# Two score products in one PSUM room, four zero fills moved to VectorE, and new instruction lists, in a gated linear attention with a maxout feed-forward block

## The chip, the cores and the metric

The kernel runs on one core of one Trainium2 chip. The core has five engines that each work through their own instructions in order: TensorE (PE in the profile, its weight loads as PEld), VectorE (DVE), ScalarE (ACT), GpSimd (POOL) and SyncE (SP, which here only issues transfers). Matrix products leave TensorE through PSUM; everything else stands in SBUF. The metric is the device time of one execution in microseconds (us), the median over runs.

## The reference

Everything is float32. Four sequences, eight heads, 768 steps, 48 channels per head; then 3072 tokens of width 384 and a hidden width of 768.

```python
mag = np.sqrt(a_re * a_re + a_im * a_im)
scale = np.minimum(mag, 0.999) / (mag + 1e-06)
a_re_n, a_im_n = (a_re * scale, a_im * scale)
...
for t in range(S):
    new_re = ar * S_re - ai * S_im
    new_im = ar * S_im + ai * S_re
    S_re, S_im = (new_re + kv, new_im)
    y[:, :, t] = np.einsum('bhd,bhde->bhe', q[:, :, t], S_re)
...
h = np.maximum(np.maximum(x @ w1, x @ w2), x @ w3)
return (h @ w_out).astype(np.float32)
```

## The kernel before

The 768 steps are cut into 12 groups of 64 (numbers 0 to 11). Each group has two tiles, x and y; a tile holds two of the four sequences with their eight heads, 128 rows of (sequence, step). Within a group the recurrence is turned into products of decayed queries and keys; between groups a state (`g`) is carried on.

The work of a group is cut into small steps, each with a short name. `SCHEDULE` is one list of 1750 such words, `name:group`, and the kernel is written out by going through it. The helper class `Bound` (line 198 is its call, so nearly every instruction of the profile has that line) ties each instruction to the one before it on its engine. So the list alone fixes the order on every engine, on the SP queue and on the POOL queue; only the waits between the engines follow from the data. Transfers are words of the list too: `Lr` and `Li` load the two parts of the gate, `Lk`, `Lq`, `Lv` keys, queries and values, `WL` the weights, `D` stores a result, and `Cd` and some others add one buffer onto another by a POOL transfer.

The words that matter below:

- `sqr`, `sqi`, `add`, `lnL`, `expe` ... `atan`, `turn`: the gate, elementwise, on ScalarE and VectorE; `af` is an absolute value.
- `sums`, `cs`, `F`: sums over steps on TensorE; `t`, `nf`, `Ek`, `Eq`, `f0` to `f3` read them out of PSUM.
- `uk`, `uq`, `tpk`, `tpq`, `Kc`, `Qc`: decayed keys and queries, their transposes on TensorE, and the copies out of PSUM.
- `A`: the scores of a tile by 32 matmuls. Head h has 80 columns, beginning at column 128 h of a PSUM room of two banks (four heads a bank).
- `g0` to `g3`: four masked copies of `A` into the tile `atm` by VectorE, one after the other.
- `B`: the scores between the halves of a chunk, by 16 matmuls with factored keys and queries (`KB`, `QB`), 128 columns; `b0`, `b1`: two ScalarE copies each from there into `atm`, behind the masked copies.
- `y`: the products of `atm` and the state with values and queries; `xx`, `xy` copy them out.
- `U`, `u`: the feed-forward products and their maximum; `S1` to `S4`, `P1` to `P7`, `r`, `o`: the output product by a Strassen scheme of seven products.
- `W..`, `T`, `M`, `J`, `O`: work at the beginning on the weights, and the output product of group 0.

PSUM is used as four rooms of two banks (a tile of 128 x 2 x 512 floats). `banks` takes the next digit of the string `SLOTS`, in list order, as the room. A room is taken over as soon as the last reader of its previous content is through. `A` takes a room for each tile and `B` takes one for both tiles of a group (in group 0 one for each tile): 258 digits.

Words in the set `OTHER` run on the engine other than the usual one: copies and absolute values on VectorE in place of ScalarE, additions on VectorE in place of a POOL transfer, loads on the POOL queue in place of SP.

Before the list begins, the kernel fills constants. In two of the `uk` tiles and both `uq` tiles the 16 columns 48 to 63 of each head's 112 are set to zero by ScalarE, as a product of a constant by 0 (line 1031); two value tiles are set to zero by VectorE.

Of the kernel before, what the change touches and what calls it, by code (L numbers as in the profile page):

```python
# [26 lines left out]
Wf6:0 nfx:0 Wb9:0 lnL:1 Enx:0 Lvy:0 csy:0 expw:1 xor:1 T2:0 relu:1 Wc9:0 We9:0 ty:0 nfy:0 mkx:0 expe:1 Wa10:0 Wf9:0
Lvx:0 Wb10:0 abs:1 Wa11:0 afx:0 sax:0 sbx:0 sumsy:0 T0:0 t0:0 mqx:0 t2:0 pw:1 Lky:1 Wb11:0 WL1:0 Lry:2 Wc10:0 half:1
Wc11:0 We10:0 ukx:0 We11:0 uqx:0 lnw:1 T1:0 Lix:2 expL:1 Wf10:0 Wa1:0 Liy:2 Wf11:0 tpqx:0 Qcx:0 mulw:1 Wb1:0 afy:0
mulai:1 tpkx:0 Wc1:0 t1:0 Fy:0 Kcx:0 kEnx:0 We1:0 WL2:0 Cdy:0 Q2x:0 Eny:0 Wf1:0 Lqx:1 lne:1 f2y:0 Q1x:0 Cdx:0 M0:0  # L30
sqi:2 Wa2:0 stt:1 Eky:0 Eqy:0 WL4:0 Wb2:0 Wa4:0 Wc2:0 Lrx:2 Wb4:0 f3y:0 We2:0 Lnop:1 f1y:0 f0y:0 say:0 Ax:0 Lqy:0
mqy:0 dkx:0 Wf2:0 g0x:0 sqr:2 sby:0 atan:1 Wg1:0 add:2 Wc4:0 lnL:2 h1x:0 QBx:0 M1:0 Lky:0 g1x:0 relu:2 turn:1 g2x:0
Wg2:0 mky:0 g3x:0 uky:0 cs:1 expe:2 WL5:0 We4:0 expw:2 M2:0 t:1 KBx:0 nfx:1 abs:2 Wa5:0 lne:2 m1:0 m0:0 uqy:0 Wb5:0
Wf4:0 Lix:3 Liy:3 Bx:0 tpqy:0 WL7:0 nfy:1 b0x:0 Wc5:0 F:1 b1x:0 sumsx:1 tpky:0 Wg4:0 xor:2 We5:0 f3:1 Qcy:0 Q1y:0 yx:0
Kcy:0 Enx:1 xx:0 Wf5:0 Q2y:0 U11x:0 Ekx:1 Eqx:1 f2:1 half:2 KBy:0 QBy:0 addw:2 Ay:0 g0y:0 Lnop:2 sumsy:1 g1y:0 f0:1
lnw:2 u11x:0 Z3:0 expL:2 f1:1 kEny:0 g2y:0 Wa7:0 af:1 Lkx:1 Wb7:0 g3y:0 Cdy:1 U01x:0 Wc7:0 mulai:2 By:0 u01x:0 b0y:0
Lqy:1 mulw:2 We7:0 Cdx:1 WL8:0 U02x:0 b1y:0 u02x:0 Wa8:0 yy:0 xy:0 sb:1 dky:0 stt:2 atan:2 h1y:0 sa:1 Wg5:0 Wf7:0
Wb8:0 U01y:0 turn:2 Wc8:0 mkx:1 U11y:0 u01y:0 u11y:0 U12y:0 Eky:1 Eny:1 mqx:1 ukx:1 U02y:0 Eqy:1 cs:2 sqi:3 uqx:1
tpqx:1 u02y:0 u12y:0 Z2:0 Lvy:1 Wg7:0 Z4:0 tpkx:1 Qcx:1 mqy:1 U21y:0 U21x:0 Lvy:2 u21y:0 We8:0 Wf8:0 Wg8:0 mky:1 Kcx:1
Q1x:1 Q2x:1 U22y:0 sumsx:2 kEnx:1 u22y:0 t:2 u21x:0 nfy:2 uqy:1 Eqx:2 Enx:2 F:2 nfx:2 Ekx:2 Ax:1 tpqy:1 f3:2 f0:2  # L40
uky:1 g0x:1 g1x:1 QBx:1 Oy:0 KBx:1 J3:0 af:2 f2:2 f1:2 Qcy:1 g2x:1 Lqx:2 mqx:2 Lvx:1 tpky:1 Q2y:1 dkx:1 QGx:1 sb:2
g3x:1 sa:2 uqx:2 Q1y:1 Lrx:3 Kcy:1 Bx:1 b1x:1 U12x:0 h0x:1 h1x:1 Lry:3 oy:0 U22x:0 b0x:1 tpqx:2 Lky:2 u12x:0 sqr:3
Qcx:2 KBy:1 Ay:1 QBy:1 u22x:0 sumsy:2 add:3 Lkx:2 g0y:1 g1y:1 g2y:1 g3y:1 Lqy:2 Eky:2 By:1 Lvx:2 yx:1 mky:2 QGy:1
kEny:1 lnL:3 xor:3 expw:3 QBx:2 xx:1 Ox:0 Eqy:2 mkx:2 Lry:4 Dy:0 expe:3 ukx:2 uky:2 b0y:1 Q1x:2 relu:3 Lrx:4 abs:3
lne:3 Lnop:3 addw:3 J1:0 Eny:2 Lqx:3 b1y:1 mqy:2 yy:1 half:3 Cdy:2 Lix:4 Cdx:2 xy:1 Liy:4 lnw:3 expL:3 J2:0 mulai:3
Lkx:3 tpky:2 kEny:2 Kcy:2 tpkx:2 Kcx:2 Lky:3 U11:1 uqy:2 u11:1 mulw:3 U01:1 tpqy:2 stt:3 atan:3 sqr:4 ox:0 h0y:1 dky:1
Q2x:2 turn:3 sqi:4 add:4 KBx:2 sumsx:3 u01:1 Qcy:2 h1y:1 cs:3 Ekx:3 h0y:2 lnL:4 Ax:2 Q2y:2 Enx:3 t:3 relu:4 kEnx:2
g0x:2 Eqx:3 Lix:5 g1x:2 nfy:3 U12:1 g2x:2 nfx:3 u12:1 g3x:2 S3:1 expw:4 U02:1 h0x:2 dky:2 af:3 F:3 expe:4 abs:4 addw:4
mqx:3 sb:3 Q1y:2 u02:1 S1:1 h1y:2 Bx:2 Lqy:3 sa:3 S2:1 Lry:5 Lvy:3 f2:3 Ay:2 b0x:2 g0y:2 P5:1 g1y:2 g2y:2 f0:3 J4:0
QBy:2 S4:1 b1x:2 P1:1 f1:3 f3:3 lnw:4 P7:1 g3y:2 QGx:2 P6:1 r1:1 sumsy:3 KBy:2 expL:4 Dx:0 r6:1 Eky:3 dkx:2 r5:1 r7:1  # L50
r57:1 Eny:3 h1x:2 By:2 yx:2 Lrx:5 xor:4 mkx:3 QGy:2 mky:3 b1y:2 ukx:3 Px:1 lne:4 Lnop:4 Eqy:3 Py:1 mqy:3 mulai:4 h0x:3
P4:1 uqy:3 uqx:3 half:4 Cdx:3 b0y:2 uky:3 P3:1 Lkx:4 Cdy:3 P2:1 xx:2 sqr:5 yy:2 xy:2 tpkx:3 Kcx:3 tpqx:3 Qcx:3 mulw:4
stt:4 U01:2 Lkx:5 Q2x:3 oy:1 Lqy:4 atan:4 Q1x:3 turn:4 ox:1 u01:2 tpky:3 QBx:3 Kcy:3 tpqy:3 F:4 Lqx:4 kEny:3 Qcy:3
QGx:3 Q1y:3 Q2y:3 sumsx:4 cs:4 f3:4 h0y:3 Liy:5 t:4 nfx:4 Ekx:4 Eqx:4 Enx:4 KBx:3 nfy:4 sqi:5 f2:4 U11:2 add:5 Ax:3
Bx:3 f0:4 Dx:1 u11:2 f1:4 lnL:5 g0x:3 mkx:4 Lvy:4 sb:4 Ay:3 mqx:4 g1x:3 af:4 g2x:3 U02:2 g0y:3 sa:4 g1y:3 g3x:3 ukx:4
relu:5 u02:2 g2y:3 Lvx:3 uqx:4 S3:2 g3y:3 KBy:3 U12:2 u12:2 b0x:3 expe:5 expw:5 kEnx:3 Lqx:6 lne:5 tpkx:4 tpqx:4 Lvx:4
dky:3 Kcx:4 S1:2 Qcx:4 dkx:3 Lky:4 sumsy:4 Eqy:4 h1y:3 S2:2 xor:5 Lry:6 Lnop:5 P1:2 Dy:1 abs:5 Eky:4 QBy:3 Lix:6 P7:2
mqy:4 P6:2 b1x:3 h1x:3 addw:5 half:5 Lrx:6 yx:3 mky:4 By:3 Eny:4 uqy:4 Cdx:4 Px:2 Py:2 lnw:5 expL:5 mulai:5 b0y:3
uky:4 Liy:6 P5:2 mulw:5 QGy:3 r1:2 xx:3 r6:2 b1y:3 S4:2 kEnx:4 P4:2 P2:2 r5:2 Cdy:4 sqr:6 sqi:6 P3:2 stt:5 atan:5
tpqy:4 Lqx:5 r7:2 r57:2 add:6 tpky:4 Qcy:4 yy:3 ox:2 dkx:4 Lix:7 Kcy:4 sumsx:5 h0x:4 turn:5 Lrx:7 Dx:2 xor:6 oy:2 xy:3  # L60
h1x:4 Q1y:4 lnL:6 Enx:5 sumsy:5 Eky:5 Ekx:5 Q1x:4 relu:6 mkx:5 cs:5 t:5 U11:3 nfx:5 expw:6 Eqx:5 Q2y:4 nfy:5 expe:6
Lky:5 mky:5 u11:3 abs:6 kEny:4 Eny:5 U01:3 af:5 Q2x:4 half:6 QGx:4 Lry:7 u01:3 Ax:4 Cdy:5 h0y:4 g0x:4 Eqy:5 g1x:4
mqx:5 dky:4 Cdx:5 F:5 g2x:4 U12:3 h1y:4 sb:5 KBx:4 QBx:4 sa:5 uqx:5 Lqy:5 U02:3 f3:5 f2:5 g3x:4 ukx:5 u12:3 uky:5
addw:6 tpqx:5 f0:5 tpky:5 u02:3 lnw:6 expL:6 f1:5 Qcx:5 Ay:4 mulai:6 Bx:4 P1:3 lne:6 Liy:7 S1:3 P5:3 mulw:6 S2:3 b1x:4
Kcy:5 g0y:4 KBy:4 b0x:4 Dy:2 sqi:7 P6:3 QBy:4 g1y:4 g2y:4 g3y:4 By:4 Lvx:5 Lky:6 mqy:5 yx:4 r1:3 S3:3 stt:6 b1y:4 P7:3
uqy:5 atan:6 tpkx:5 b0y:4 tpqy:5 QGy:4 Kcx:5 r6:3 turn:6 yy:4 Qcy:5 r5:3 r7:3 Lnop:6 sqr:7 Q1x:5 xy:4 Lkx:6 Lvy:5
h0x:5 S4:3 Q2y:5 sumsx:6 xx:4 kEnx:5 r57:3 cs:6 t:6 Ekx:6 add:7 nfy:6 Q1y:5 Py:3 nfx:6 lnL:7 P4:3 expw:7 Px:3 U01:4
QGx:5 expe:7 kEny:5 relu:7 Eqx:6 QBx:5 mqx:6 Enx:6 P2:3 af:6 Q2x:5 dkx:5 h1x:5 Liy:8 KBx:5 u01:4 sa:6 mkx:6 abs:7
sumsy:6 Eny:6 F:6 Lry:8 addw:7 oy:3 Lqy:6 U11:4 Eqy:6 P3:3 f2:6 Dy:3 f0:6 h0y:5 Eky:6 f3:6 f1:6 Bx:5 xor:7 u11:4 QBy:5
ox:3 lnw:7 sb:6 Ax:5 KBy:5 Ay:5 mqy:6 By:5 half:7 g0x:5 g1x:5 g2x:5 g3x:5 g0y:5 g1y:5 g2y:5 U02:4 Lvx:6 lne:7 b1x:5  # L70
b0x:5 yx:5 g3y:5 u02:4 expL:7 Lrx:8 mulai:7 U12:4 b1y:5 mulw:7 stt:7 Cdx:6 Lix:8 b0y:5 xx:5 atan:7 ukx:6 S3:4 P7:4
QGy:5 P1:4 tpkx:6 Kcx:6 u12:4 uqx:6 tpqx:6 Cdy:6 yy:5 mky:6 xy:5 S1:4 Qcx:6 S2:4 Dx:3 dky:5 sqi:8 r1:4 turn:7 uky:6
Q1x:6 Lnop:7 sqr:8 h1y:5 add:8 sumsx:7 kEnx:6 cs:7 t:7 P5:4 Eqx:7 P6:4 Px:4 S4:4 Py:4 P4:4 P2:4 Lvx:7 xor:8 Ekx:7
Lkx:7 P3:4 lnL:8 r6:4 uqy:6 nfy:7 r5:4 r7:4 r57:4 nfx:7 expe:8 Enx:7 tpqy:6 tpky:6 h0x:6 Lqx:7 F:7 expw:8 relu:8 mqx:7
af:7 Lvy:6 Lky:8 ox:4 Qcy:6 QBx:6 dkx:6 oy:4 Dy:4 mkx:7 Lix:9 Q2y:6 U11:5 abs:8 Dx:4 QGx:6 half:8 f0:7 Q1y:6 h1x:6
KBx:6 Kcy:6 sb:7 sa:7 f2:7 U01:5 ukx:7 U12:5 Q2x:6 kEny:6 uqx:7 f3:7 addw:8 h0y:6 u01:5 Lrx:9 u11:5 f1:7 u12:5 dky:6
# [988 lines left out]
```

## Time and profile before

| | |
|---|---|
| median of 3 timed runs | 553.96 us (553.03 to 554.14) |
| the profiled execution's own time | 549.62 us |
| its span, which the profile divides | 547.9 us |
| mean granted TensorE clock in it | 0.983 |
| transfers in it | 47.93 MB, mean 87 GB/s |

The profile page gives, for one execution, the busy time of each engine, the span in 40 slices (each digit the busy tenths of a slice), the chain of work that ended last, and groups of instructions of one kind with their count, their summed time and the mean of one. Other views of the trace give the busy time in chosen stretches, the instructions in order of time, and who waited for whom. Times count from the beginning of the span. The 1.72 us between the span and the execution's own time belong to neither engine. The rows themselves stand where the prediction uses them.

### The profile page before, as it was taken

What the parts mean: (1) busy time and instruction counts of PE and PEld (TensorE: products, weight loads), DVE (VectorE), ACT (ScalarE), POOL (GpSimd) and SP (SyncE); (2) the same over time, 40 slices, a digit from 0 to 9 for tenths busy, and PEclk for the clock granted to TensorE, in tenths of its full rate; (3) what the DMA queues carried; (4) which work ended last, traced back from release to release, by engine and by line L of the source; (5) the groups of instructions that cost most, each with busy time, mean ns of one, the idle gap of its engine ahead of it and who ended that gap; (6) DMA issues with size and microseconds to landing.
All of it is one profiled execution on the core that took longest, in us unless ns stands there. A gap on an engine that the chain in (4) does not pass through costs nothing.

```text
span 547.9 us, 22377 instructions
## 1 busy us (share of the span) xinstructions
PE 512.3 (94%) x9998; PEld 439.4 (80%) x9998; DVE 484.2 (88%) x730; ACT 367.4 (67%) x575; POOL 119.9 (22%) x173
## 2 busy tenths in 40 slices
PE   2469889999999999999999999999999999999997
...
DVE  6999989999999999999999969998999996977234
ACT  7999988779858878689585558756567578211100
...
GB/s 240 270 203 197 183 155 57 90 91 130 45 76 75 106 81 53 159 63 61 91 21 186 32 17 102 90 67 74 97 68 25 75 105 1 4 44 4 2 0 58
DMA packets 113983, 47.93 MB, mean 87 GB/s; under 512 B 100832, under 2 KB 106400, under 8 KB 113888
## 3 DMA queue, kind: packets, MB, share of 16 engines
...
q14 instruction: 17, 0.14, 0.1%
...
## 4 chain that ended last, share of the span: by engine, by line
PE 72%; DVE 12%; ACT 6%; DMA 4%; issue 3%; SPq 2%; POOL 0%; DVEq 0%; ACTq 0%
PE up L198 28%; PE op L198 22%; PE y L198 6%; PE A L198 4%; PE dk L198 3%; PE tp L198 3%; SPq L198 2%; PE sums L198 2%; DVE xhx L198 2%; ACT L198 2%; PE F L198 1%; PE cs L198 1%; PE B L198 1%; DMA q<-in_q_dram 1%; DVE uk L198 1%
## 5 line engine op out<-in xcount | busy, mean ns | idle before, releaser
L198 PE MATMUL up<-xhx,w 128*128 128x256 f32 x792 | 177.7, 382 | 0.0
L198 PEld LDWEIGHTS up<-xhx,w 128*128 128x128 f32 x792 | 148.4, 190 | 23.4 <-issue 1.2
L198 ACT ACT_TABLE_LOAD x53 | 68.0, 1283 | 4.5 <-issue 3.6
L198 POOL DMA_DIRECT2D ar<-nf x44 | 41.9, 1382 | 85.8 <-DVE ar L198 82.7
L198 PE MATMUL op<-wo,xhx 128*128 128x192 f32 (+1 forms) x220 | 49.2, 362 | 0.0
L198 DVE TENSOR_TENSOR Q<-Q,f 112x1024 f32<-112x1024 f32 (+1 forms) x48 | 44.9, 949 | 0.1
L198 ACT COPY atm<-B 32x128 f32<-32x128 f32 x96 | 24.6, 256 | 29.9 <-DVE atm L198 22.8
L198 PE MATMUL y<-atm,vb 128*32 128x64 f32 x1152 | 39.0, 221 | 0.8 <-issue 0.8
L198 PEld LDWEIGHTS op<-wo,xhx 128*128 128x128 f32 x220 | 36.7, 190 | 3.4 <-ACT xhx L198 0.6
L198 DVE TENSOR_TENSOR xhx<-xhx,up 128x768 f32<-128x768 f32 x22 | 20.9, 950 | 19.7 <-PE up L198 19.6
L198 PEld LDWEIGHTS y<-atm,vb 128*32 128x32 f32 x1152 | 32.9, 109 | 5.0 <-issue 3.1
L198 PE MATMUL y<-QG,g 112*32 112x64 f32 x1408 | 36.7, 218 | 0.0
L198 DVE TENSOR_TENSOR ot<-ot,op 128x192 f32<-128x192 f32 (+1 forms) x66 | 27.1, 416 | 9.7 <-PE op L198 7.0
L198 PEld LDWEIGHTS y<-QG,g 112*32 112x32 f32 x1408 | 34.3, 109 | 0.0
L198 PE MATMUL op<-wo,strassen 128*128 128x192 f32 x176 | 32.9, 330 | 0.0
L198 PE MATMUL op<-w,strassen 128*128 128x192 f32 x176 | 32.5, 329 | 0.3 <-issue 0.3
L198 PE MATMUL A<-Q,K 112*32 112x80 f32 x1536 | 30.8, 234 | 1.4 <-issue 1.3
L198 DVE COPY_PREDICATED atm<-masko,A 128x256 f32<-128x256 uint8 x72 | 30.2, 432 | 1.3
L198 PEld LDWEIGHTS A<-Q,K 112*32 112x32 f32 x1536 | 27.3, 110 | 4.8 <-issue 3.1
L198 ACT ACTIVATE xhx<-up 128x768 f32<-128x768 f32 x16 | 13.0, 811 | 27.0 <-PE up L198 27.0
L198 PEld LDWEIGHTS op<-w,strassen 128*128 128x128 f32 x176 | 29.0, 190 | 2.0 <-issue 1.0
L198 PEld LDWEIGHTS op<-wo,strassen 128*128 128x128 f32 x176 | 28.9, 190 | 1.7 <-ACT e L198 0.6
...
## 6 DMA issues: line engine op xcount, KB each, us to landing
...
```

The lines of the kernel that those rows point to most:

```text
L198: ins = f(*a, **kw)
```

## The change

Four edits, made together:

1. `B` no longer has a room. `A` and `B` of a tile share one, taken by whichever of the two comes first in the list. `B` writes the 32 columns behind the 80 of `A`, for the four heads of the first bank, and `b0`, `b1` read them there.
2. The four zero fills are VectorE memsets.
3. `SCHEDULE` is another list of the same 1750 words, and `SLOTS` another string, of 245 digits.
4. `OTHER` is another set.

```diff
@@ scores
         if name == "A":
-            ps = T["A", x] = banks("A")
+            ps = once(("A", x), lambda: banks("A"))
...
         elif name == "B":
-            g, c_ = divmod(x, C)
-            ps = T["B", x] = once(("Bp", g if g > 0 else -x), lambda: banks("B"))[:, c_:c_ + 1]
+            ps = once(("A", x), lambda: banks("A"))
...
-                        mm(out=ps[o:o + 32, 0, i * 32:i * 32 + 32], lhsT=T["KB", x][0:DD, 2 * h + j],
+                        mm(out=ps[o:o + 32, 0, i * P + 80:i * P + 112], lhsT=T["KB", x][0:DD, 2 * h + j],
...
-            src = T["B", x][:, 0, 0:4 * 32].rearrange("p (h t) -> p h t", h=4)
+            src = T["A", x][:, 0].rearrange("p (h t) -> p h t", h=4)[:, :, 80:112]
@@ before the list
     for t in us["k"][:2] + us["q"]:
-        act.mul(t[:, :, D:L64], biases[:, 0:1].to_broadcast([P, H * (L64 - D)]).rearrange("p (h d) -> p h d", h=H), 0.0)
+        dve.memset(t[:, :, D:L64], 0.0)
@@ SCHEDULE, its first words
-Lrx:0 sqr0:0 Lix:0 Zf:0 CL:0 sqi0:0 add0:0 Liy:0 sqi1:0 Zg:0 lnL0:0 Lry:0 WL0:0 sqr1:0 add1:0 expe0:0 expw0:0 lne0:0
+Zf:0 Lix:0 sqi0:0 Lrx:0 Lry:0 sqr0:0 sqr1:0 add0:0 lnL0:0 Liy:0 sqi1:0 Zg:0 xor0:0 WL0:0 xor1:0 WL3:0 expe0:0 expw0:0
...
@@ OTHER
-abs0:0 Lkx:0 Lqy:1 Lqx:1 Wg4:0 Wg8:0 Lkx:2 Lqx:3 Lvy:1 abs:3 addw:3 Lkx:3 Lky:3 Lvy:3 u11:2 addw:5 Lvy:4 Lvx:5 Lqx:5
-u01:3 abs:6 Lvy:5 Lkx:6 u11:4 Lvx:6 Lvy:6 addw:7 Qcx:6 Lky:6 Lkx:7 u11:5 af:7 u01:5 Lky:7 xx:6 Kcx:7 af:8 Lqx:8 Kcy:7
-Lqx:9 xx:7 xy:7 u01:7 af:9 abs:10 Lvx:8 Lqx:10 Lvx:9 af:10 Lqx:11 Qcy:9 Lvx:10 abs:11 Kcx:10 Lqy:10 xx:9 Lkx:11 Lvy:10
-xx:10 xy:10 Qcy:11 Kcx:11 Lvy:11 Kcy:11
+abs0:0 Lkx:0 Lqx:0 afx:0 Lvx:0 Wg4:0 Lqy:1 u01x:0 Lvy:1 Wg8:0 Lqx:2 Lvx:2 Lqy:2 addw:3 af:3 Lqy:3 Lkx:3 Lqx:4 af:4
+Lvy:3 Lqx:6 Lvx:3 Lqx:5 Lkx:5 abs:6 addw:6 af:5 Lqy:5 Kcx:5 Lkx:6 af:6 addw:7 Lky:6 Qcy:6 af:7 addw:8 u11:5 xx:6 Lvy:8
+af:8 Lky:8 Lvx:8 xx:7 Qcy:8 u11:7 Lkx:9 af:9 Lvy:9 Lqy:10 Lvx:9 abs:11 xx:9 addw:11 Lky:11 Lky:10 af:11 xx:10 Kcy:11
+Lvx:11
```

Of the new lists the change says that they were made for several draws of the times at which transfers land. Old and new differ nearly everywhere in the order of single words; the products that TensorE computes are the same. Where `B` stands among the masked copies, in list order:

| tile | before | after |
|---|---|---|
| x of group 0 | A g0 g1 g2 g3 B | A g0 g1 g2 B g3 |
| y of group 4 | A g0 g1 g2 g3 B | A g0 g1 g2 B g3 |
| y of group 6 | A g0 g1 g2 g3 B | A g0 g1 B g2 g3 |
| y of group 10 | A g0 g1 g2 g3 B | A g0 B g1 g2 g3 |
| x of group 4 | A g0 g1 g2 g3 B | B A g0 g1 g2 g3 |
| x of group 8 | A g0 g1 B g2 g3 | B A g0 g1 g2 g3 |

Over all 24 tiles of the changed list, `B` stands behind at least one masked copy of its own tile in 12, and ahead of all of them in the other 12.

More of the change, by code (lines that the diff above doesn't have):

```diff
@@ L27 @@
[L27 to L76, printed above, removed]
@@ new lines @@
+Ax:1 g0x:1 g1x:1 g2x:1 g3x:1 uky:1 mqx:2 tpqy:1 Ekx:2 Qcy:1 Oy:0 sqi:3 Lrx:3 Q1y:1 QBx:1 Lry:3 Q2y:1 af:2 tpky:1 sb:2
+QGx:1 dkx:1 Lky:2 KBx:1 oy:0 Bx:1 kEny:1 h0x:1 Kcy:1 U12x:0 b1x:1 KBy:1 U22x:0 h1x:1 QBy:1 b0x:1 Lqy:2 mkx:2 sa:2
+u12x:0 sqr:3 Ay:1 uqx:2 By:1 add:3 ukx:2 u22x:0 g0y:1 g1y:1 xor:3 lnL:3 relu:3 expw:3 yx:1 sumsy:2 Eqy:2 Eky:2 Eny:2
+expe:3 g2y:1 mky:2 g3y:1 lne:3 abs:3 Ox:0 Lky:3 b1y:1 QGy:1 mqy:2 tpqx:2 uqy:2 Lnop:3 half:3 uky:2 Lrx:4 b0y:1 yy:1
+Qcx:2 tpky:2 tpqy:2 ox:0 J3:0 xy:1 tpkx:2 addw:3 Cdy:2 Q1x:2 Cdx:2 xx:1 J1:0 lnw:3 expL:3 Q2x:2 kEny:2 mulw:3 Kcx:2
@@ new lines @@
+xor:4 Lvx:3 mulai:4 By:2 Eky:3 half:4 mulw:4 yx:2 stt:4 Eqy:3 sa:3 sb:3 xx:2 Px:1 P3:1 Cdy:3 b0y:2 QGy:2 Cdx:3 Py:1
+b1y:2 P2:1 atan:4 mky:3 sqi:5 Eny:3 P4:1 ukx:3 uqx:3 mqy:3 yy:2 xy:2 tpkx:3 Kcx:3 tpqx:3 uqy:3 U01:2 Qcx:3 oy:1 u01:2
+uky:3 QGx:3 turn:4 ox:1 Q1x:3 tpqy:3 Qcy:3 tpky:3 Kcy:3 kEnx:3 QBx:3 h0y:3 F:4 f3:4 sumsx:4 Q2y:3 cs:4 f2:4 Lrx:5
+Lkx:5 f1:4 h0x:3 sqr:5 Ekx:4 Q2x:3 t:4 f0:4 nfy:4 KBx:3 Lkx:4 nfx:4 Enx:4 Eqx:4 Q1y:3 sb:4 af:4 kEny:3 Dy:1 sa:4 Lvy:4
+U11:2 Lqx:4 mqx:4 Bx:3 add:5 Ax:3 lnL:5 Ay:3 g0x:3 mkx:4 u11:2 U02:2 g0y:3 g1x:3 expw:5 expe:5 g1y:3 relu:5 ukx:4
@@ new lines @@
+u02:2 g2x:3 g2y:3 lne:5 U12:2 g3x:3 S3:2 b0x:3 abs:5 Lry:6 uqx:4 Lky:4 b1x:3 tpkx:4 Kcx:4 addw:5 u12:2 Lix:6 xor:5
+tpqx:4 Qcx:4 dky:3 g3y:3 sumsy:4 Eky:4 Lvx:4 dkx:3 h1y:3 P7:2 Eny:4 S1:2 mky:4 KBy:3 S2:2 P5:2 P6:2 half:5 P1:2 Lqy:4
+QBy:3 h1x:3 kEnx:4 lnw:5 expL:5 S4:2 r1:2 By:3 Dx:1 b1y:3 Lrx:6 yx:3 b0y:3 Lnop:5 Px:2 P2:2 Py:2 mulw:5 mulai:5 Eqy:4
+uky:4 P4:2 r6:2 r5:2 QBx:4 r7:2 QGy:3 stt:5 P3:2 Lqy:5 tpky:4 Cdy:4 atan:5 Cdx:4 mqy:4 r57:2 sqr:6 uqy:4 Lqx:5 oy:2
+tpqy:4 Qcy:4 yy:3 Lky:5 KBx:4 Kcy:4 dkx:4 turn:5 xx:3 ox:2 xy:3 sumsy:5 Liy:6 h0x:4 kEny:4 sumsx:5 h1x:4 Eny:5 Enx:5
```

123 lines of the change are left out of this document (79 added, 44 removed).

## The prediction

> **What bounds the kernel now.** First the page: its totals and its slices.
>
> ```profile
> span 547.9 us, 22377 instructions
> PE 512.3 (94%) x9998; PEld 439.4 (80%) x9998; DVE 484.2 (88%) x730; ACT 367.4 (67%) x575; POOL 119.9 (22%) x173
> ...
> PE   2469889999999999999999999999999999999997
> DVE  6999989999999999999999969998999996977234
> ACT  7999988779858878689585558756567578211100
> ```
>
> TensorE is full from the seventh slice on. Ahead of that VectorE and ScalarE are full and TensorE is not. VectorE stays at nine tenths to the middle. The view of stretches, cut at two places that I explain next, gives the idle time:
>
> ```profile
> 0.00:14.00 14.00, 3.09 (x36) 2.15 (x37) 9.75 (x27) 9.90 (x21) 11.20 (x41) 1.00 0.90 241
> 14.00:84.80 70.80, 52.65 (x824) 36.40 (x823) 68.47 (x105) 67.78 (x110) 25.90 (x30) 0.88 0.93 199
> 84.80:237.70 152.90, 151.00 (x3372) 129.63 (x3376) 148.61 (x218) 120.72 (x184) 36.79 (x46) 1.00 0.45 87
> 237.70:540.00 302.30, 301.73 (x5750) 267.69 (x5751) 254.24 (x378) 169.01 (x263) 46.04 (x57) 1.00 0.28 56
> 540.00:547.90 7.90, 3.86 (x24) 3.56 (x22) 3.09 (x7) 0.00 (x0) 0.00 (x0) 0.92 0.19 51
> ```
>
> The columns are the length, then the busy time of PE, PEld, DVE, ACT and POOL. From 84.8 to 540 us TensorE is idle for 2.5 us in all. Nothing but later or earlier readiness of its inputs can move the end, and what is lost ahead of 84.8 us is lost for good. VectorE's idle time is 4.25 us in the first 14, 2.33 in the next 70.8, 4.29 to 237.7: 10.9 together, so up to there it is almost a second bound. Behind 237.7 it idles 48 us.
>
> The two cuts are checkpoints. In both lists the same TensorE words stand ahead of `tpqx:1` (transposes of tile x, group 1) and again ahead of `sumsx:6`, in other orders. As the products are the same, the time at which these two begin says how the kernels stand.
>
> **The change part by part.**
>
> *The zero fills.* In order of time, with the piece of the chain of waits that leads in:
>
> ```profile
> 1.58 3.84 DMA ai<-in_a_im_dram
> ...
> 4.92 0.51 ACT L198 ACTIVATE uk<-biases 128x128 f32<-128x128 f32 x2
> 5.33 0.49 ACT L198 ACTIVATE uq<-biases 128x128 f32<-128x128 f32 x2
> 5.73 0.51 ACT L198 ACTIVATE e<-ar 128x384 f32<-128x384 f32 x1
> 6.68 0.66 DVE L198 CUSTOM_DVE_ANT_0 L<-L,e 128x384 f32<-128x384 f32 x1 [2.62 <-ACT L L198]
> 7.08 0.52 ACT L198 ACTIVATE L<-ai 128x384 f32<-128x384 f32 x1 [0.43 <-DMA ai<-in_a_im_dram]
> 7.51 0.51 ACT L198 ACTIVATE L<-L 128x384 f32<-128x384 f32 x1
> ```
>
> The four products take ScalarE 0.81 us (4.92 to 5.73). But the first square of the new list needs `ai`, which lands at 1.58 + 3.84 = 5.42; the third needs SP's third load, for which ScalarE waited until 7.08; the logarithm behind it starts at 7.5 as before. So removing them gains nothing, and ScalarE's idle start grows by 0.81. On VectorE the four memsets, 0.17 each by a memset of the same size (row below), lie in the 2.62 us ahead of 6.68. Without that cover they would cost 0.66. The first addition comes some 0.3 earlier (5.42 + 2 x 0.46 for two squares = 6.3).
>
> *ScalarE to the first checkpoint.*
>
> ```profile
> 81.53 0.65 ACT L198 ACTIVATE hT<-up 128x256 f32<-128x256 f32 x2
> 84.25 0.50 ACT L198 ACTIVATE E<-sums 128x384 f32<-128x384 f32 x1
> ...
> 83.40 0.94 DVE L198 TENSOR_TENSOR uq<-CS,q 128x768 f32<-128x768 f32 x1
> 84.80 0.66 PE L198 MATMUL tp<-ident,uq 64*112 64x64 f32 x16 [0.20 <-ACT E L198]
> ```
>
> The transposes start at 84.80, when `Eqy:1` on ScalarE frees their room (ends 84.75); `uqx:1` on VectorE ended at 84.34. In the old order 133 ScalarE instructions stand ahead of this point, in the new one 125. Gone are the four fills (covered, nothing), `afx:0` (0.51 by the square of that size) and `u01x:0` (0.33, half of the first row), both now VectorE's; and `Eky:1` and `Eqy:1`, two exponentials that now stand behind the checkpoint (0.4 each, as they follow one another). Sum 0.51 + 0.33 + 0.8 = 1.6 us sooner.
>
> *VectorE to both checkpoints.* Its rows:
>
> ```profile
> L198 DVE COPY_PREDICATED atm<-masko,A 128x256 f32<-128x256 uint8 x72 | 30.2, 432 | 1.3
> L198 DVE COPY_PREDICATED atm<-maskd,A 128x512 f32<-128x512 uint8 x24 | 17.4, 728 | 2.1 <-PE A L198 2.1
> L198 DVE TENSOR_TENSOR w<-w,L 128x768 f32<-128x768 f32 x13 | 12.4, 950 | 0.7 <-ACT L L198 0.7
> L198 DVE CUSTOM_DVE_ANT_0 L<-L,e 128x768 f32<-128x768 f32 (+1 forms) x13 | 11.7, 899 | 3.0 <-ACT L L198 2.6 <-issue 0.4
> L198 DVE SCALAR_TENSOR_TENSOR w<-w,ar 128x768 f32<-128x768 f32 (+1 forms) x13 | 11.6, 890 | 1.3 <-DMA ar<-nf 1.3
> L198 DVE TENSOR_TENSOR strassen<-xhx,strassen 128x512 f32<-128x512 f32 x11 | 7.5, 683 | 7.5 <-PE op L198 7.5
> L198 DVE COPY K<-tp 112x1024 f32<-112x1024 f32 x5 | 6.1, 1216 | 0.3 <-PE tp L198 0.3
> L198 DVE TENSOR_SCALAR xhx<-up 128x768 f32<-128x768 f32 x6 | 5.6, 946 | 0.0
> L198 DVE TENSOR_TENSOR hT<-hT,up 128x256 f32<-128x256 f32 x6 | 2.4, 409 | 0.0
> L198 DVE TENSOR_SCALAR af<-nf 128x768 int32<-128x768 int32 x4 | 2.2, 552 | 0.0
> L198 DVE TENSOR_SCALAR L<-ar 128x768 int32<-128x768 int32 x4 | 2.2, 550 | 0.0
> L198 DVE MEMSET upto<- 128x128 f32 x1 | 0.2, 165 | 0.0
> ```
>
> To `tpqx:1` VectorE gets `afx:0` (0.28, half of an `af`), `u01x:0` and `u12y:0` (0.41 each) and loses one weight step (about 0.55): +0.55, less 0.3 for the earlier start. If none of its later waits shrank it would be ready at 84.34 + 0.3, and the gain would be 0.2 us; if they do, ScalarE's 1.6 is the limit. Range 0.2 to 1.6.
>
> To `sumsx:6` the new order has these ahead that the old one has not: four memsets (0.66, in idle time), `afx:0` 0.28, `u01x:0` 0.41, `af:3 af:4 af:5` 1.66, `addw:6` 0.95, `S4:3` 0.68, `turn:6` 0.89, `add:7` 0.90, `Kcx:5` 1.22: 7.7. Not ahead any more: `abs:3` 0.55, `u11:2` 0.95, `addw:5` 0.95, `u01:3` 0.95: 3.4. Net 4.3, and I take 4.0 since each starts a little before the one ahead of it ends. How near was VectorE?
>
> ```profile
> 234.45 1.22 DVE L198 TENSOR_TENSOR QG<-Q,f 112x1024 f32<-112x1024 f32 x1
> ...
> 235.94 1.72 PE y L198 x112
> 237.66 0.81 PE sums L198 x16
> ```
>
> The last that counted was `QGy:4`, ending at 235.67, with `yy:4` (1.72) still between it and the sums. In the new order it is `Kcx:5`, directly ahead of the sums. So they gain 237.6 - 235.67 = 1.9 of room. Start: 235.7 + 4.0 = 239.7, less the covered memsets and the earlier start (0.66 + 0.3): 238.7, which is 1.1 later than before. Against that stand waits of VectorE up to here:
>
> ```profile
> DVE atm L198 <- PE A L198: 1.5, 1, 1.5
> DVE nf L198 <- ACT t L198: 1.2, 2, 1.0
> ```
>
> Both are for engines that were late because ScalarE was. With ScalarE 1.6 sooner I take 2.3 of these 2.7 us as gone: 238.7 - 2.3 = 236.4, 1.2 us sooner than 237.6. Bounds: 1.1 later with none gone; ScalarE's 1.6 sooner.
>
> *Behind it.* TensorE is idle 0.6 us in the next 302, so the difference stays. VectorE has 48 idle us there, and the new `OTHER` takes work off it (relu by `xhx<-up` six to two, `K` copies five to two). At the end both lists finish with the last product, one addition and a store:
>
> ```profile
> 543.89 0.56 DVE L198 TENSOR_TENSOR ot<-ot,op 128x384 f32<-128x384 f32 x1 [0.56 <-PE op L198]
> ```
>
> Nothing changes there. The leftover `kEny:11` stood behind that addition, beside the store; its successor `kEnx:11` stands ahead of it, in idle time.
>
> *The shared room.* Thirteen fewer rooms are taken. But the built order of the changed kernel has waits that the old one lacks: where `B` stands behind a masked copy, its first matmul waits for that copy, and the next copy waits for `B`, although the columns are different. In-order TensorE then holds all products behind `B`. The copies of a tile take 0.73 + 3 x 0.43 = 2.02 us; `B` stands behind at least one of them in 12 tiles. I take 0: in six of the 12, eleven or more words of the list lie between the copy and `B`, and in the other six one to five; only those six are near. Bounds: 0, and one copy in each, 12 x 0.43 = 5.2.
>
> [...]
>
> **The sum.** 547.9 - 1.2 = 546.7 for the span, 549.62 - 1.2 = 548.4 for that execution. The median of the runs shown is 4.3 us above the profiled one; I carry the difference over: 553.96 - 1.2 = 552.8.
>
> **The rivals.**
>
> *VectorE takes ScalarE's place* and none of its waits shrink: +1.1, 555.1. For it: 68.47 of 70.80 and 148.61 of 152.90 us busy, and +4.0 of work moved forward. Against: its waits for the scores and for `t` are ScalarE's lateness.
>
> *Slower: `B` locked to the masked copies.* In 12 tiles TensorE stops for one copy: 5.2 - 1.2 = +4.0, 558.0. It decides from six such tiles on (6 x 0.43 = 2.6 eats the gain and the margin). For it: a VectorE with under 3% idle time reaches its copies late. Against: the distance in the list, which leaves just six near cases.
>
> *Landing times.* The timed runs take 4.3 us more than the profiled one, and transfers are 0.90 and 0.93 busy in the first two stretches. If that excess is waiting for transfers, and the new list is proof against it: 549.6. For it: the chain passes a landing of over five us in the second stretch.
>
> ```profile
> 38.97 5.53 DMA ar<-in_a_re_dram
> ```
>
> Against: ScalarE and VectorE were busy for all but 3.0 and 2.3 of the 70.8 us there, so the landing cost them little.
>
> *The change doesn't do what it says:* the freed rooms and the new order only move the waits about, 553.96.
>
> **How the numbers follow.** Forecast 0.36 (its own range 551.8 to 553.6), VectorE 0.26, locked `B` 0.16, landing times 0.14, nothing 0.08. Within 0.2% (1.1 us), what a measurement here can't tell from no change, lie a quarter of the forecast, a third of the VectorE case and the last: 0.09 + 0.09 + 0.08 = 0.26. Faster: 0.27 + 0.14 = 0.41. Slower: 0.17 + 0.16 = 0.33. The range goes from just under the landing case to just under the locked one, 549.2 to 557.8.
>
> **What would show it.** Right: `tpqx:1` begins at 83.2 to 84.6 and `sumsx:6` near 236.4, VectorE's idle time up to there falls from 10.9 us, and the first addition on VectorE stands at about 6.4 with the memsets ahead of it. Wrong: `sumsx:6` at 238.7 or later with VectorE idle as before; or waits of `A<-QB,KB` for `atm` on VectorE in a dozen tiles; or a gain that arises behind 237.7 us, where I see none.

## The result, and the profile after

| | before | after |
|---|---|---|
| median of 20 timed runs each | 552.32 us (550.71 to 554.46) | 556.02 us (551.49 to 559.24) |
| the profiled execution's own time, and its span | 549.62, 547.9 | 552.38, 550.5 |

The ratio is 1.0062, with a 95% interval of 1.0042 to 1.0082: slower, by 3.7 us between the medians, where the forecast was 1.2 us faster. The spread has changed too: these 20 runs of the kernel before lie within 4 us, those of the changed one cover 8.

The stretches of the changed kernel, cut where the prediction cut them (the columns are again the length, then the busy time of PE, PEld, DVE, ACT and POOL):

```profile
0.00:14.00 14.00, 3.11 (x36) 2.18 (x37) 10.17 (x31) 9.34 (x17) 11.20 (x41) 1.00 0.89 236
14.00:84.80 70.80, 53.66 (x827) 37.26 (x828) 68.52 (x107) 67.12 (x107) 27.57 (x33) 0.86 0.93 201
84.80:237.70 152.90, 149.62 (x3304) 128.57 (x3306) 149.00 (x217) 118.52 (x183) 38.38 (x48) 1.00 0.43 84
237.70:540.00 302.30, 300.75 (x5818) 266.18 (x5807) 247.66 (x371) 175.31 (x271) 41.51 (x49) 1.00 0.28 54
540.00:550.50 10.50, 6.13 (x36) 5.56 (x34) 4.09 (x8) 0.00 (x0) 0.00 (x0) 0.99 0.14 38
```

TensorE's idle time in the third stretch is 3.28 us (1.90 before), in the fourth 1.55 (0.57 before). VectorE's up to 237.7 is 3.83 + 2.28 + 3.90 = 10.0 us (10.9 before). What ended TensorE's idle time behind 84.8 us, by the view of waits (us in total, how often, the longest):

```profile
PE y L198 <- issue: 2.4, 2, 1.5
PE A L198 <- issue: 0.6, 1, 0.6
PE tp L198 <- PE y L198: 0.5, 1, 0.5
PE A L198 <- DVE KB L198: 0.4, 1, 0.4
PE up L198 <- issue: 0.3, 1, 0.3
```

The large ones are not for another engine. "issue" is time in which the engine waited for nothing that the profile shows. In the timeline such a stop can lie inside a word, between two products of the same kind, where the trace shows no wait for an input:

```profile
67.97 0.73 PE L198 MATMUL F<-cuts,Ln 64*48 64x29 f32 x46
73.56 0.60 PE L198 MATMUL F<-cuts,Ln 64*48 64x29 f32 x18 [4.85 <-issue]
```

These are two rows of `F:1` from a second profiled execution of the changed kernel (first experiment below). In the first execution the same word breaks after the same 46 products, and `yx:1` breaks at 106.8:

```profile
68.20 0.73 PE L198 MATMUL F<-cuts,Ln 64*48 64x29 f32 x46
70.49 0.41 PE L198 MATMUL F<-cuts,Ln 64*48 64x29 f32 x18 [1.56 <-issue]
...
106.78 0.22 PE L198 MATMUL y<-QG,g 112*32 112x64 f32 x1
108.47 0.24 PE L198 MATMUL y<-QG,g 112*32 112x64 f32 x1 [1.47 <-issue]
```

What sits at these places? The page's part on DMA queues has a row that the prediction passed over:

```profile
q8 instruction: 78, 1.28, 0.9%
```

78 packets, 1.28 MB: 16384 bytes each in the trace. TensorE's stream in the trace (products, weight loads and the sequencer's own rows, in order of time) has 20126 instructions, 258 for each packet. Numbering the stream shows that behind 84.8 us every one of these stops stands at an instruction whose number is 193 plus a multiple of 256. I call these places boundaries. One stretch between two of them:

```profile
218.30:231.50 13.20, 12.62 (x255) 11.02 (x255) 12.86 (x20) 11.16 (x18) 1.55 (x2) 1.00 0.44 85
```

255 products and 255 weight loads; with two rows of the sequencer they are 512, two blocks of 256. Five of the stops and the packets on that queue, worked out from the first profile (times in us):

```
instruction   last start   next start   packet before it: begins, takes   next start behind its end
  1217          68.73        70.49        68.09   0.88                       1.52
  2753         106.78       108.47       106.24   0.99                       1.24
  7617         217.63       218.34       216.00   0.93                       1.41
  8129         230.77       231.57       229.30   0.92                       1.35
 16321         430.45       431.63       429.15   0.99                       1.49
```

These numbers fit instructions of TensorE that come in blocks of 256, each by one packet (0.88 to 1.51 us in this profile, 0.96 in the median). That of a block begins only around the time at which TensorE passes the boundary before it: in these five rows 0.9 to 3.2 us behind it, elsewhere in this profile up to 4.0 ahead. In the five rows TensorE went on 1.24 to 1.52 us after the packet had ended. The blocks that end at these five stops hold dense words (in this profile 112 products of `y` start within 1.7 us, 64 of `A` in 1.1) and lasted 2.5 to 4.1 us: they were used up before the next one was there. I call these stops fetch stops, and count one where at a boundary the gap between two starts is over 0.25 us and over the usual spacing of such products, and the packet ended 1.1 to 2 us before.

In this profile 7 of 78 boundaries stop TensorE. They cost it 6.95 us, and the experiments show lists in which such stops cost far more (up to 30.3 us, with 128 instructions ahead).

### The profile page after: what moved, and what is told of

Same layout as the page of the kernel before. It is cut to its first block, busy times and chain, and to the rows that moved or that the text cites. A ratio compares the mean times of both kernels' runs of the same rounds, so it can differ in the third digit from the quotient of the medians.

```text
span 550.5 us, 22367 instructions
## 1 busy us (share of the span) xinstructions
PE 513.3 (93%) x9998; PEld 439.8 (80%) x9998; DVE 479.4 (87%) x730; ACT 370.3 (67%) x575; POOL 118.7 (22%) x169
## 3 DMA queue, kind: packets, MB, share of 16 engines
q8 instruction: 78, 1.28, 0.9%
## 4 chain that ended last, share of the span: by engine, by line
PE 80%; DVE 8%; ACT 4%; issue 3%; DMA 2%; SPq 2%; ACTq 0%; DVEq 0%
PE up L198 32%; PE op L198 22%; PE y L198 7%; PE A L198 6%; PE tp L198 4%; PE dk L198 4%; SPq L198 2%; PE sums L198 2%; PE F L198 1%; DVE xhx L198 1%; DVE Q L198 1%; DVE w L198 1%; PE cs L198 1%; DMA xhx<-in_moe_w_out_dram 1%; DVE atm L198 1%
## 5 line engine op out<-in xcount | busy, mean ns | idle before, releaser
L198 PE MATMUL up<-xhx,w 128*128 128x256 f32 x792 | 177.4, 382 | 0.4 <-issue 0.3
L198 PEld LDWEIGHTS up<-xhx,w 128*128 128x128 f32 x792 | 148.6, 190 | 23.4 <-DVE g L198 1.3
L198 POOL DMA_DIRECT2D ar<-nf x44 | 44.3, 1471 | 58.0 <-DVE ar L198 56.1
L198 DVE TENSOR_TENSOR Q<-Q,f 112x512 f32<-112x512 f32 (+1 forms) x48 | 44.8, 953 | 4.4 <-ACT Q L198 4.4
L198 PE MATMUL op<-wo,xhx 128*128 128x192 f32 (+1 forms) x220 | 48.7, 363 | 0.0
L198 ACT COPY atm<-A 32x128 f32<-32x128 f32 x96 | 24.5, 256 | 34.3 <-DVE atm L198 29.9
L198 PEld LDWEIGHTS op<-wo,xhx 128*128 128x128 f32 x220 | 36.8, 190 | 5.7 <-ACT xhx L198 0.9
L198 PE MATMUL y<-atm,vb 128*32 128x64 f32 x1152 | 39.5, 221 | 1.0 <-issue 1.0
L198 DVE TENSOR_TENSOR xhx<-xhx,up 128x768 f32<-128x768 f32 x22 | 20.9, 950 | 20.6 <-ACT xhx L198 11.1
L198 PE MATMUL y<-QG,g 112*32 112x64 f32 x1408 | 37.1, 218 | 1.5 <-issue 1.5
L198 PEld LDWEIGHTS y<-atm,vb 128*32 128x32 f32 x1152 | 33.1, 109 | 4.8 <-issue 4.0
L198 PEld LDWEIGHTS y<-QG,g 112*32 112x32 f32 x1408 | 34.4, 109 | 1.6 <-issue 1.6
L198 DVE TENSOR_TENSOR ot<-ot,op 128x192 f32<-128x192 f32 (+1 forms) x66 | 27.1, 418 | 8.8 <-PE op L198 6.3
L198 POOL DMA_DIRECT2D Ln<-e x11 | 14.2, 1294 | 94.9 <-ACT e L198 88.4
L198 ACT ACTIVATE xhx<-up 128x768 f32<-128x768 f32 x20 | 16.1, 807 | 27.0 <-PE up L198 26.9
L198 DVE COPY_PREDICATED atm<-masko,A 128x256 f32<-128x256 uint8 x72 | 30.8, 435 | 2.4 <-PE A L198 1.3
L198 PE MATMUL op<-wo,strassen 128*128 128x192 f32 x176 | 32.7, 328 | 0.0
L198 PE MATMUL op<-w,strassen 128*128 128x192 f32 x176 | 32.5, 329 | 0.0
L198 ACT ACTIVATE E<-sums 128x384 f32<-128x384 f32 x48 | 22.6, 491 | 13.8 <-PE sums L198 9.9
L198 PE MATMUL A<-Q,K 112*32 112x80 f32 x1536 | 30.3, 234 | 1.7 <-ACT K L198 1.5
L198 PEld LDWEIGHTS op<-wo,strassen 128*128 128x128 f32 x176 | 29.1, 190 | 1.5 <-issue 0.8
```

The costliest lines, as they stand in the source:

```text
L198: ins = f(*a, **kw)
```

## The experiments

Theory F in what follows: the loss is made of fetch stops. Its rivals change from run to run and are named in the expectations. "Small products" are matmuls of 3 x 3 elements on a constant, which put four instructions each into TensorE's stream: with 32 of them the page counts 10062 products and 10062 weight loads, 64 more of each. The edit for 32:

```diff
+    pad = psum.tile([P, 2, 512], FP, tag="ps3", name="pad")
+    for _ in range(32):
+        mm(out=pad[0:3, 0, 0:3], lhsT=biases[:, 0:3], rhs=biases[:, 0:3], start=True, stop=True)
     program(SCHEDULE, 0)
```

**The changed kernel again** (no edit).

> The changed kernel once more, for a second profiled execution and its spread beside the others. Theory F (instruction fetch): in the first profile TensorE stopped 6.7 us in all (before: 2.6) at instructions 193 + 256 j of its stream, in the middle of words, where a transfer of 16 KB on the instruction queue had ended only 1.2 to 1.5 us earlier. Then the same boundaries (tiles F near 70.5, yx:1 near 108, U02:3 near 218, By:4 near 231, yx:9 near 431, tpqx:11 near 485) stop again, by amounts that differ by tenths, 6 to 10 us in all, and the ratio is 1.004 to 1.008. Theory W (late inputs): the stops are waits for VectorE or ScalarE that the profile failed to name; then they come and go with those engines and are not bound to the instruction's number.

Measured: 1.0043 (1.0013 to 1.0073), 550.8 to 558.9 us. This profile fell on a long execution: 558.89 us, span 557.1. It stops at six boundaries, 11.75 us in all, against 6.95 at seven in the first. Five of the six expected places stop again (not the one near 485, which stands in `tpkx:11` and not in `tpqx:11`), and there is a new stop of 1.7 us at 280. The stop in `F:1` is 5.06 us instead of 1.76. The two executions differ by 6.6 us in span, and 4.8 of it are fetch stops.

**128 instructions ahead of either list** (the edit above, on the changed kernel and on the one before).

> The changed kernel with 32 products of 3 x 3 elements ahead of everything on TensorE, at a time when it idles: they cost nothing by themselves, and move the boundaries of the 256-instruction blocks by 128 instructions. Theory F: no stop where the stops were (108, 218, 231, 431); new ones in the middle of words near 105.5, 139, 148, 171, 199.5, 212, 224, 233 and some ten later places, since 23 blocks instead of 12 now last less than 3.3 us; the time is 3 to 9 us longer than the changed kernel's, 1.011 to 1.022 of the kernel before. Theory W: the stops stay in their words, and the time is the changed kernel's within 0.3%.

> The kernel before with the same 32 products ahead. Theory F: 25 blocks instead of 11 last less than 3.3 us, so 3 to 9 us longer, 1.006 to 1.016. Theory W: 1.000 within 0.002.

Measured: 1.0443 (1.0402 to 1.0485) and 1.0483 (1.0454 to 1.0512), some 20 and 26 us more than the same lists without the small products. The sign and most of the places are Theory F's, the size is more than twice what it expected at most. The waits of the padded new list:

```profile
PE A L198 <- issue: 8.3, 8, 1.4
PE y L198 <- issue: 4.4, 4, 1.9
PE dk L198 <- issue: 3.4, 3, 1.3
PE F L198 <- issue: 2.3, 2, 1.2
PE tp L198 <- issue: 1.8, 1, 1.8
```

They have moved to other words. `F:1`, which broke after 46 products, is whole, and a later word, `By:0`, breaks instead:

```profile
68.53 0.92 PE L198 MATMUL F<-cuts,Ln 64*48 64x29 f32 x64
...
72.38 0.34 PE L198 MATMUL A<-QB,KB 112*32 112x32 f32 x17 [0.58 <-DVE atm L198]
74.48 0.33 PE L198 MATMUL A<-QB,KB 112*32 112x32 f32 x15 [1.76 <-issue]
```

There are 24 fetch stops, 30.3 us, in the padded new list, and 18 stops, 25.6 us, in the padded old one.

**256 instructions ahead** (64 small products on the changed kernel). If the small products themselves cost, this costs more than 32 of them; if the boundaries do, they are back in place.

> The changed kernel with 64 of the small products ahead: 256 instructions, one whole block, so that the boundaries fall where the changed kernel has them, one block later in number. Theory F: the stops are back at yx:1, By:4, the words of 270 to 280 us, yx:9, four to seven in all, 5 to 12 us; 1.004 to 1.009 of the kernel before, though twice as many products stand ahead as in the run with 32 (1.044). Rival C (the small products themselves, or the time TensorE starts, are what costs): more than with 32, 1.04 to 1.09.

Measured: 1.0127 (1.0087 to 1.0167), against 1.0443 with half as many. Nine stops, 8.2 us in the profiled execution (555.65 us), and `F:1` breaks again after 46 products:

```profile
70.56 0.73 PE L198 MATMUL F<-cuts,Ln 64*48 64x29 f32 x46
72.08 0.45 PE L198 MATMUL F<-cuts,Ln 64*48 64x29 f32 x18 [0.79 <-issue]
```

The ratio is above Theory F's 1.009 and far below the rival's 1.04. With this it is shown that the places of the boundaries set the loss: half a block ahead costs one and the same list some 20 us, a whole one 4. What the 4 are made of is open.

**12 instructions ahead** (3 small products, on the changed kernel and on the one before).

> The changed kernel with 3 of the small products ahead instead of 32: the boundaries move by 12 instructions. From the durations of the blocks alone the stops would be about a tenth less than the changed kernel's (sum of shortfalls below 3.9 us per block 18.1 instead of 20.0). Theory F: same places as the changed kernel, or one word earlier, 0.5 to 2 us less, 1.000 to 1.007. If 12 instructions already cost as much per instruction as 128 did: 1.008 or more, which would mean that the small products themselves cost and not the boundaries.

> The kernel before with 3 of the small products ahead, 12 instructions. By the durations of its blocks this is near its best place (sum of shortfalls below 3.9 us 11.7 instead of 16.1). Theory F: the stop near 70 us (1.5 to 2.8) goes or shrinks, and nothing over 1 us comes in its place: 0.995 to 1.000. Rival C: 1.001 to 1.005.

Measured: 1.0029 (1.0009 to 1.0048) for the changed kernel, 549.95 to 554.89 us, and 1.0060 (1.0039 to 1.0081) for the one before. In the first `F:1` is whole and there is no fetch stop ahead of 84.8 us; 7.7 us remain behind:

```profile
68.43 0.92 PE L198 MATMUL F<-cuts,Ln 64*48 64x29 f32 x64
```

The times no longer reach to 559. So the stop in `F:1`, 1.0 to 5.1 us in six profiles of lists that have it there, probably makes much of the changed kernel's spread. The second was a miss: the early stop stayed at 1.5, and two of 1.3 and 0.9 came at 146 and 278. The durations of blocks alone, from which I had expected a gain, foretell the sign of the large step of 128 but not single stops.

**Words moved** (four places in the list of the changed kernel).

```diff
-dky:4 U02:3
+U02:3 dky:4
-By:4 uqy:5 xx:4 atan:6 g3y:4 b1y:4 Lvx:5 sqr:7 P6:3
+P6:3 By:4 uqy:5 xx:4 atan:6 g3y:4 b1y:4 Lvx:5 sqr:7
-yx:9 S1:8 S2:8 f0:10 xx:9 P6:8
+S1:8 S2:8 f0:10 P6:8 yx:9 xx:9
-U12x:0 b1x:1 KBy:1 U22x:0 h1x:1 QBy:1 b0x:1 Lqy:2 mkx:2 sa:2 u12x:0 sqr:3 Ay:1 uqx:2 By:1
+b1x:1 KBy:1 h1x:1 QBy:1 b0x:1 Lqy:2 mkx:2 sa:2 sqr:3 Ay:1 uqx:2 By:1 U12x:0 U22x:0 u12x:0
```

> The changed kernel with seven words of its list moved by a few places, so that a word with long products stands inside the block of 256 instructions that ends in a stop: U12x:0 and U22x:0 (with u12x:0) from ahead of Ay:1 to behind By:1 (stop of 1.7 us near 108), U02:3 ahead of dky:4 (0.7 near 218), P6:3 ahead of By:4 (0.8 near 231), P6:8 ahead of yx:9 and xx:9 (1.2 to 1.7 near 431). Work and engines are the same. Theory F: these four stops, 4.4 to 5.0 us, shrink to under 1.5 in all, and the time falls by 2 to 5 us, to 0.995 to 1.001 of the kernel before. Rival S (the new order itself is the loss: late VectorE, held rooms): the stops change their place but the time stays at 1.003 to 1.008.

Measured: 1.0098 (1.0061 to 1.0135). All four stops are gone: behind 84.8 us 0.9 us of stops remain, of 5.2 and 6.7 in the two profiles without the moves. But the time did not fall. Waits for other engines stand in their place:

```profile
PE A L196 <- ACT atm L196: 1.2, 1, 1.2
...
PE up L196 <- DVE g L196: 1.1, 1, 1.1
...
PE op L196 <- DVE strassen L196: 1.2, 1, 1.2
```

(The first rows of the view of waits for 84.8 to 130, 215 to 232 and 425 to 445 us; L196 is the line L198 of the other kernels.) The span less its fetch stops is 550.8 us, over 5 more than without the moves. This run can't tell the theories apart: a word moved by a few places meets inputs that aren't there yet. A smaller move, one word, on top of the 3 small products:

```diff
-P7:4 u12:4 h0y:5 tpqx:6 tpkx:6 Lix:9 Kcx:6 yy:5
+u12:4 h0y:5 tpqx:6 tpkx:6 Lix:9 Kcx:6 yy:5 P7:4
```

> The changed kernel with 3 of the small products ahead (1.0029 by itself, with stops of 1.8 and 1.6 us near 274 and 278) and one word, P7:4, moved from ahead of tpqx:6 to behind yy:5, so that eight long products stand between the short ones there. Theory F: these two stops shrink to under 0.5 each, if the transposes that now come 1.4 us earlier don't wait for VectorE: 0.997 to 1.000 of the kernel before. If they do wait, the time is as without the move, 1.001 to 1.005.

Measured: 1.0049 (1.0028 to 1.0069). One of the two stops is gone (278), the other (1.7 at 274) is not, and the time is no better. No version made here beats the kernel before.

**Small products at the end** (320 of them behind the last word; a single execution).

> The changed kernel with 320 of the small products behind its last word, when no load is under way: 1280 instructions, five blocks, on a TensorE that has nothing else. Theory F: they don't run at their own rate (256 of them in under 2 us) but at the rate of the fetches, one stop per block, 3.5 to 4.5 us for each, 15 to 22 us in all. Theory W: no stop among them, 7 to 10 us in all.

Measured: no stop among them. The 1280 instructions take 16.1 us, 3.2 us a block, and that is their own rate: the products start 50 ns apart, at a granted clock of 0.65 in the first half of that stretch and 0.50 in the second. So the time lies in Theory F's range without the stops that were to make it, and above Theory W's. The run was meant to be dense and wasn't; it tells only that in this stretch, at 3.2 us a block and with no load under way, the transfers kept up. The queue has 83 packets, five more than without the five blocks, so it is TensorE's.

**The first two edits by themselves.** The fills alone, in the kernel before:

> The kernel before with the zero fills alone, by VectorE. The prediction's cost of this edit: 0, hidden in VectorE's 2.62 us of idle time and ScalarE's wait for its input: 0.999 to 1.001. The other end of its bounds: 0.66 us later, 1.001. TensorE's instructions are the same, so Theory F has its stops where the kernel before has them.

Measured: 0.9998 (0.9980 to 1.0016). The shared room and the fills, in the old lists:

```diff
+            if g in (3, 4, 9):
+                ps, w, o_ = once(("Bp", g), lambda: banks("B"))[:, c_], 32, 0
+            else:
+                ps, w, o_ = once(("A", x), lambda: banks("A"))[:, 0], P, 80
```

`SLOTS` keeps 226 of its digits; the rest had to change because rooms are now held at other times.

> The old lists, unchanged, with the first two edits alone: the zeroes by VectorE, and the second score product in the free columns of the first one's room, in nine of the twelve groups (in groups 3, 4 and 9 the old order leaves no room free, so they keep the room of their own). Instructions on TensorE stay the same in number and order. Theory F, and the prediction's cost of 0 for both edits: 0.999 to 1.002. The rival that the second score product is locked to the masked copies: 9 tiles' worth of 0.43 us, 1.003 to 1.008, with waits of TensorE for atm.

Measured: 1.0363 (1.0342 to 1.0384), 20 us more. Its fetch stops are 5.7 us, so most of the loss has another source. TensorE's waits behind 84 us:

```profile
PE A L196 <- DVE atm L196: 6.1, 3, 3.1
PE tp L196 <- DVE ot L196: 2.1, 2, 1.9
PE y L196 <- ACT Q L196: 1.6, 1, 1.6
...
PE tp L196 <- ACT atm L196: 1.2, 1, 1.2
PE tp L196 <- ACT K L196: 1.1, 1, 1.1
```

The first fits TensorE at a room that the masked copies still read; rows of `tp` waiting for what others write fit rooms that come free late. How much is the shared room and how much the changed digits was not separated.

**A weight load issued later** (the word `WL5` from ahead of `g0x:0` to behind `F:1`, with its steps and those of `WL8` behind it), to find out why the packet ahead of `F:1`'s break is so late.

> The changed kernel with one weight load of 768 KB, WL5, issued some 6 us later in the list (behind F:1 instead of ahead of g0x:0, 64.8 us in the first profile), and the steps that use it and the load WL8 behind it moved back with it. TensorE's list is untouched, so the boundaries stay in their words. Theory L (the fetch of the block that ends in F:1 is late because loads fill the transfer engines, share 1.00 to 1.03 behind the boundary near 64): the share there falls, the fetch begins under 2 us behind the boundary instead of 3.2 and 6.8 us, and the stop in F:1, 1.8 and 5.1 us in two profiles, is under 0.8. Rival: the fetch is late for another reason, then the stop in F:1 stays between 1.5 and 5 us. In both, later weights can cost some us near 100 us, where U12x:0 and U22x:0 need them, so the whole time tells little: 0.998 to 1.012.

Measured: 1.0372 (1.0350 to 1.0395); the load was issued at 82.9 us, 18 later than in the changed kernel and not 6, and the late weights cost 11.9 and 6.8 us at two products, as the expectation had feared but not sized. For the question itself: the stop in `F:1` is still 1.65 us, a miss for Theory L. The stretches behind the boundary at 63.6 (the last two columns are the transfer engines' share and GB/s):

```profile
64.50:65.00 0.50, 0.50 (x7) 0.50 (x7) 0.50 (x1) 0.50 (x2) 0.00 (x0) 1.00 1.24 240
65.00:65.50 0.50, 0.48 (x5) 0.29 (x3) 0.50 (x2) 0.50 (x1) 0.00 (x0) 1.00 1.05 203
65.50:66.00 0.50, 0.29 (x16) 0.29 (x20) 0.50 (x2) 0.50 (x3) 0.00 (x0) 1.00 0.73 135
66.00:66.50 0.50, 0.50 (x41) 0.50 (x34) 0.50 (x2) 0.50 (x3) 0.00 (x0) 1.00 0.02 0
```

Even without `WL5` the transfer engines are full to 65.9, and the packet begins at 66.5. In the 557.1 us execution they are full past 70.6, and it begins at 70.68. That fits a packet that waits behind loads, as does the delay of packets behind their boundary: up to 7.4 us between 53 and 75 us, 0.8 in the median behind 90 us. Against it, in the run with one word moved and 3 small products the packet began only 0.5 us behind the boundary at 63.8, though the transfer engines were full (1.09 and 1.44 in the half microseconds on either side). So why the packets are late is open; no run here had that stretch free of loads.

**The profiles of the two lists together** (those with words moved, rooms changed or products at the end left out). The span less the fetch stops:

| profile | span | fetch stops to 84.8, behind | the rest |
|---|---|---|---|
| old list | 547.9 | 1.5, 0.6 | 545.7 |
| old list, fills by VectorE | 551.4 | 2.8, 0.5 | 548.1 |
| old list, 3 small products | 551.8 | 1.5, 2.5 | 547.8 |
| old list, 32 | 575.9 | 5.6, 20.1 | 550.2 |
| new list | 550.5 | 1.8, 5.2 | 543.5 |
| new list, again | 557.1 | 5.1, 6.7 | 545.3 |
| new list, 3 | 552.9 | 0, 7.7 | 545.2 |
| new list, 64 | 553.9 | 1.5, 6.7 | 545.7 |
| new list, 32 | 575.9 | 4.1, 26.2 | 545.6 |

With 7 to 30 us of stops the rest of the new list stays within 2.2 us: in it a stop is lost nearly in full, as TensorE is the bound. The rest of the old list is less steady, 545.7 to 550.2. In every row the rest of the new list is no longer than the shortest of the old one, and in the mean of the two profiles each without small products it is 2.5 us shorter; with so few profiles that is a rough size.

## Why the prediction was wrong

*The zero fills, nothing:* right, 0.9998. But the first addition was not 0.3 us earlier; it begins at 6.72 (6.68 before), as `ai` landed at 1.58 + 4.09 = 5.67 instead of 5.42:

```profile
1.58 4.09 DMA ai<-in_a_im_dram
...
6.72 0.61 DVE L198 CUSTOM_DVE_ANT_0 L<-L,e 128x384 f32<-128x384 f32 x1 [2.10 <-ACT e L198]
```

*ScalarE to `tpqx:1`, 0.2 to 1.6 us sooner, begin at 83.2 to 84.6:* it began at 84.66.

```profile
84.66 0.66 PE L198 MATMUL tp<-ident,uq 64*112 64x64 f32 x16
...
238.75 0.56 PE L198 MATMUL sums<-Ln,mid 64*64 64x192 f32 x8
```

1.76 us of fetch stops lie ahead of it, and 1.49 ahead of the old one. Less the stops, it lies at 82.9, 84.6 and 83.9 in three profiles of the new list (the second of them the repeat, the third with 3 small products) and at 83.3, 85.5 and 84.2 in three of the old one (unchanged, with the fills by VectorE, with 3 small products): half a microsecond sooner in the mean, in the lower half of the range.

*VectorE to `sumsx:6`, 236.4:* it began at 238.75, the very number of the VectorE rival (238.7). The cause is not the rival's. 4.96 us of stops lie ahead of it (2.14 in the old list); less the stops it lies at 233.8, 235.5 and 235.3 in the same three profiles, and at 235.5, 237.7 and 237.3 in the three old ones: about 1.9 us sooner, where I had said 1.2. The waits that I took as gone are gone: of VectorE's 1.5 us for the scores and 1.2 for `t`, between 14 and 237.7 us, 0.2 each are left, 2.3 of 2.7 less as assumed, though a new one of 1.1 heads the view:

```profile
DVE hT L198 <- PE up L198: 1.1, 1, 1.1
...
DVE nf L198 <- ACT t L198: 0.2, 1, 0.2
...
DVE atm L198 <- PE A L198: 0.2, 1, 0.2
```

The sign I had named for "wrong", 238.7 with VectorE idle as before (10.0 us now, 10.9 then), could not tell a late VectorE from a TensorE that stops by itself. A sign has to name the row, not just the time.

*Behind it, "the difference stays":* this is the step that failed, together with the begin of `sumsx:6`, and for one reason. The sum took the same products in another order to last as long, and the prediction said that nothing but the readiness of its inputs can move TensorE's end. TensorE idled 1.0 us more in that stretch in the first profile, where three fetch stops lie, and in the second 3.4 us of stops lie behind 237.7. The term that the sum lacked is the change of the fetch stops: +4.8 us between the two unpadded first profiles (6.95 against 2.14), +8.4 with the second of the new list against the fills-only one (11.75 against 3.33). With the gain of 2.5 that gives +2.3 to +5.9. This is no independent check, as the 2.5 comes from the same four profiles, whose spans differ by 2.6 and 5.7; measured between the medians of the timed runs, 3.7. The old list's profile had shown the term, as rows of "issue" that the prediction did not look at: 1.49 us between two starts in the middle of `Ay:0` at 70.2 and 0.65 in the middle of `P7:1` at 145.

```profile
67.95 1.02 PE L198 MATMUL A<-Q,K 112*32 112x80 f32 x45
70.23 0.61 PE L198 MATMUL A<-Q,K 112*32 112x80 f32 x19 [1.26 <-issue]
...
145.35 1.95 PE L198 MATMUL op<-w,strassen 128*128 128x192 f32 x11 [0.32 <-issue]
```

That the measured 556.0 lies inside the stated 549.2 to 557.8, and near the 555.1 of the VectorE rival, is luck: no term and no rival had these stops.

*The end:* the last addition and the store take 4.3 us behind the last product, 4.0 before; nothing changed there beyond tenths, as said.

*The shared room, 0 in bounds of 0 to 5.2:* right for the changed kernel, where TensorE waits for a masked copy once, ahead of 84.8, for 1.0 us, and has no such row behind:

```profile
PE A L198 <- DVE atm L198: 1.0, 1, 1.0
```

In the old order the bounds would not have held (6.1 us for masked copies alone, with the changed digits). So it seems to be the new list that pays for the shared room; a gain by the room itself was not seen. The list can put other products between a masked copy and `B`.

*The rivals:* the locked `B` and a late VectorE are out, by the rows above. "Landing times" had the new list proof against transfers. If the loads do delay the packets, they are what widens its spread: the opposite.
